# Three due times in a routed attention and gated feed-forward kernel: one pair's loads, one head's one-hot copies, one head's logits

## The chip, the cores and the metric

The kernel runs on one core of one Trainium2 chip. The metric is the device time of one execution in microseconds; the median of three runs is the time of the kernel. In the text, TensorE (PE) does the matmuls, VectorE (DVE), ScalarE (ACT) and GpSimd (POOL) the elementwise work, and SyncE (SP) issues nearly all transfers.

## The reference

```python
q_n, k_n, c_n = (x / (norm(x) + 1e-6) for x in (q, k, centroids))
q_assign = argmax(einsum("bhsd,hcd->bhsc", q_n, c_n), -1)    # 16 clusters a head
k_assign = argmax(einsum("bhsd,hcd->bhsc", k_n, c_n), -1)
mask = q_assign[:, :, :, None] == k_assign[:, :, None, :]
scores = where(mask, q @ k.T / sqrt(64), -1e9)
attn = softmax(scores)                                        # 4 batches, 8 heads, 768 tokens, 64
x = (attn @ v).transpose(0, 2, 1, 3).reshape(3072, 512)
out = (sigmoid(x @ w_gate) * (x @ w_val)) @ w_out             # 512 -> 1536 -> 512
```

Inputs and output are float32. A token attends only to tokens of its head that fall to the same cluster.

## The kernel before

**The mask is part of the score matmul.** For each head a tile `T` holds, for 6 chunks of k and 6 of q, the transposed rows: 64 rows of the values rounded to float16 (`hi`) and 64 rows of what the rounding left (`lo`). `hi` and `lo` together give the cluster logits (`logits`, L354 to L368), on which the cluster is picked (`pick`, L376 to L391): a maximum, a one-hot row for k, and for q a row of -1920 wherever the cluster is not its own. Once the logits of a head are read, 16 of the `lo` rows (64 to 79) are overwritten with these one-hot rows. A score matmul with 80 rows then gives q.k, less 1920 times the mismatch, and an exponential on ACT (L598) makes the weights `es`; an `av` matmul (L611) multiplies them with v and a column of ones.

**How one pair of heads is prepared** (`pair_prep`, L1118 to L1176; in the second, third and fourth batch). SP loads k, q and v of the pair, 384 KB each (`load`, L180). For head e: `sp` casts to `hi` on DVE and subtracts to `lo` on POOL, into a tile `hl` (L1125, L1126); `tn` lets SP issue a DMA transpose of `hl` into `T` (L341); `lg` runs twelve logits matmuls on TensorE (L361), after which ACT or DVE copies one half of them out (`lglo`, L367); `pk` joins and picks on DVE (L373, L382 to L391). When both heads are picked, `ot` issues a DMA transpose of the one-hot tile into `ohT` (L1143), and `hp0` and `hp1` each issue two small copies of 24 KB, from `ohT` into rows 64 to 79 of one head's `T` (`hop`, L412). The score matmuls of the pair need these.

**The order is written by due times.** The attention runs as 384 steps, 96 a batch, each a score matmul of one k chunk against 384 tokens (128 x 384), its exponential, and the `av` of a step two or three earlier. In the second batch head 0 of the third pair begins at step 144, in the third batch the pairs begin at steps 192, 216, 240 and 264. All preparation is put under a due time, the step at which the pair is used plus an offset from the table `SCHED`:

```python
def at(i, f):
    bg.setdefault(max(i, step_no[0] - 0.5), []).append(f)

def run_bg(i):
    for x in sorted(x for x in bg if x <= i):
        for f in bg.pop(x):
            f()
```

`run_bg` is called twice in each step, after the scores and after the `av`. So a due time fixes where an instruction stands in the program and thereby in the in-order list of each engine and queue; it is no wait. What an instruction waits for are its data and the release of the buffer that it writes.

**Between the steps** the feed-forward of 384 tokens that are ready is spread over the steps (`ffn_run`, a budget of ns a step): four matmuls of `g` (L427) and a tanh on ACT (L433), four of `v` (L443) and a product `hT` on DVE (L448), and at the end of a block the matmuls of `o` (L461). Scores, `g`, `v`, logits and `vs_ps` share a ring of four PSUM banks: a new one waits until the bank that it gets has been read out.

**The edited entries,** with their steps before: `b2ld` with `b2lk`, `b2lq`, `b2lv` (loads of all pairs of the third and fourth batch; for the third batch's second pair steps 133, 133.5 and 134.5 for k, q and v), `b1p2hp0` (144 - 10.5 = 133.5; its neighbour `b1p2hp1` stands at 129.5), `b2lg0` and `b2pk0` (for the third batch's first pair 192 - 39 = 153). The transpose of that pair's head 0, `b2tn0`, is due at step 142.

Of the kernel before, what the change touches and what calls it, by code (L numbers as in the profile page):

```python
# [9 lines left out]
HP = mybir.dt.float16  # L10
# [73 lines left out]
}  # L84
# [3 lines left out]
def kernel(  # L88
# [15 lines left out]
    DM = out.shape[1]  # L104
# [10 lines left out]
    PARTS = [(sum(SIZES[:i]), n) for i, n in enumerate(SIZES)]  # L115
    Q0 = SIZES[0]
    NB = 128 * max([3] + SIZES)
    BASE = [0] + [48 * NPT + 96 * (b - 1) for b in range(1, B)]
# [36 lines left out]

    warm = const.tile([128, 512], HP, name="warm")
    POOL.memset(warm, 0.0)
# [37 lines left out]
    def load_half(eng, side, part):  # L195
        if part == 0:
            RAW[side, 0, 0] = raw(side)
        c = slice(3 * part, 3 * part + (3 if side == "k" else Q0))
        eng.dma_start(out=RAW[side, 0, 0][:, 0, c], in_=view(side, 0, 0)[:, 0, c])

    ACT.dma_start(out=cen, in_=centroids.rearrange("h c d -> (h c) d"))
    load_half(SP, "k", 0)
    load_half(ACT, "q", 0)
    load_half(SP, "k", 1)
    load_head(SP, "k", 0, 1)
    load_head(SP, "q", 0, 1, slice(0, Q0))

    WQ = 6
    wg, wv = [], []
    for i in range(NFC // WQ):  # L210
        wg.append(wpool.tile([128, NDC, WQ, 128], HP, name=f"wg{i}"))
        wv.append(wpool.tile([128, NDC, WQ, 128], HP, name=f"wv{i}"))
    wo = [wpool.tile([128, NFC // 2, DM], HP, name=f"wo{i}") for i in range(2)]

# [8 lines left out]
    def load_wo(i):  # L223
        done.add(("wo", i))
        POOL.dma_start(
            out=wo[i],
            in_=moe_w_out.rearrange("(g fc p) m -> p g fc m", g=2, p=128)[:, i],
        )
# [37 lines left out]

    def v_cast(b, p, cast=None):
        done.add(("v", b, p))
        va = VA[b, p] = vas[(b * NP + p) % len(vas)]
        (cast or POOL.tensor_copy)(va[:, :, :, 0:64], RAW["v", b, p])  # L270

# [24 lines left out]

    def v_sum_pe(b, p):
        t = (turns if SCHED.get("lgop", 1) else bank)(130, FP, name="vs_ps")
        for j in range(NCH):
            PE.matmul(  # L300
                out=t.rearrange("p (h d) -> p h d", h=2), lhsT=ones, rhs=VA[b, p][:, :, j, :],
                start=(j == 0), stop=(j == NCH - 1),
            )
        sv = svp.tile([128, 2, 65], FP, tag="sv", name="sv")
        SV[b, p] = sv
        DVE.tensor_scalar(sv.rearrange("p h d -> p (h d)"), t, TINY, None, ALU.mult)
# [35 lines left out]

    def logits2(groups):

        lg = (turns if SCHED.get("lgop", 1) else bank)(512, FP, name="lg2")
        for i, (t, c, h) in enumerate(groups):
            for s in range(2):
                PE.matmul(  # L348
                    out=lg[:, bass.ts(i, NCL)], lhsT=t[:, c, :], rhs=cm[:, h, s, :],
                    start=(i == 0 and s == 0), stop=(s == 1), skip_group_check=True,  # L350
                )
        return lg[:, 0 : len(groups) * NCL].rearrange("p (c n) -> p c n", n=NCL)
# [64 lines left out]
    def ffn_atoms(xT, t0, n, b, ch, final=False):  # L417
# [36 lines left out]
        def outp(t, part, st):  # L454
            def f():
                if part == 0:
                    need(("wo", 0), ("wo", 1))
                    st.append(op.tile([128, DM], FP, tag="o", name="o"))
                o = st[0]
                for fc in range(4 * part, 4 * part + 4):  # L460
                    PE.matmul(  # L461
                        out=o, lhsT=hT[:, fc, bass.ts(t, 128)], rhs=wo[fc // 6][:, fc % 6, :],
                        start=(fc == 0), stop=(fc == NFC - 1),
                    )
# [23 lines left out]
        def closing(t, a, z):  # L488
            def f():
                w = z - a  # L490
                o = bank(w, name="o_end")
                for fc in range(NFC):
                    PE.matmul(  # L493
                        out=o, lhsT=hT[:, fc, bass.ts(t, 128)],
                        rhs=wo[fc // 6][:, fc % 6, a:z],
                        start=(fc == 0), stop=(fc == NFC - 1),
                    )
                ob = osp.tile([128, w], FP, tag="ob_end", name="ob_end")
                if a:
                    DVE.tensor_scalar(ob, o, 0.5, None, ALU.mult)  # L500
                else:
                    ACT.activation(ob, o, AF.Copy, scale=0.5)
                SP.dma_start(
                    out=out[b * S : (b + 1) * S].rearrange("(p c) m -> p c m", c=NCH)[
                        :, ch[t], a:z
                    ],
                    in_=ob,
                )

            return f  # L510
# [90 lines left out]
    def do_av(s):  # L601
        b, p, e, nq = s["b"], s["p"], s["e"], s["nq"]
        first, last = s.get("first", False), s.get("last", False)
        need(("v", b, p))
        if first:
# [58 lines left out]
    def dummies(n, m=512):  # L664
# [3 lines left out]
        for i in range(n):  # L668
            PE.matmul(out=w[:, 0:m], lhsT=warm[:, 0:128], rhs=warm[:, 0:m], start=True, stop=True)

    def pieces(b, p, e, parts=1):
# [107 lines left out]
        return dict(hi=hi, lo=lo, tu=tu, ev=ev, lg=lg, pk=pk, ot=ot, pl=pl)  # L779

    def first(p, e, parts=1):

        h, st = 2 * p + e, {}

        def rng(s, part):
            n = NCH // parts
            return (6, 6 + Q0) if s else (n * part, n * part + n)

# [47 lines left out]
        def lg(part=0):  # L836
# [4 lines left out]
            else:  # L841
                st["lg", part] = logits2(gs)

        def pk(part=0):
# [4 lines left out]
            DVE.tensor_reduce(mx[:, 0:n], lg_, AX.X, ALU.max)  # L849
            m = NCH // parts  # L850
            for s, x, y in ((0, 0, m), (1, m, n)):
                if x == y:
                    continue
                o = m * part if s == 0 else 0
                v_ = oh_view(ohx[0, p], 2 * e + s, 1, 1, 6)[:, 0, o : o + y - x]
# [6 lines left out]
        def ot(part=0):  # L862
            if SCHED.get(f"hO{p}", 0):
# [6 lines left out]
                return  # L870
            n = NCH // parts
            m = n if part else max(n, Q0)
            ps = st["oh", part] = turns(128 * m, name="oh_ps")
            for c in range(m):
                PE.transpose(ps[:, bass.ts(c, 128)], ohx[0, p][:, n * part + c, :], identh)  # L875

        def pl(s, eng=None, part=0):
            a, z = rng(s, part)
            if SCHED.get(f"hO{p}", 0):
                need(f"h{2 * p + 1}ot")  # L880
                hop(ohy[0, p], 2 * e + s, T[0, h], a, z - a)
                return
            src = st["oh", part][64 * e + 32 * s : 64 * e + 32 * s + 16, 0 : 128 * (z - a)]
            dst = T[0, h][64:80, a:z, :].rearrange("p c t -> p (c t)")
# [103 lines left out]
    for x in SCHED.get("lo", ["v0", "k1", "q1", "v1", "k2", "q2", "v2", "k3", "q3", "v3"]):  # L988
        if x[0] == "q":
            load_chunks(SP, "q", int(x[1]), 0)  # L990
# [4 lines left out]
    a, b_ = P[0, 0, 0], P[0, 0, 1]  # L995
    a["hi"](0, None, 0)
    a["hi"](1, ACT.copy, 0)
    a["lo"](0, DVE, 0)
    a["lo"](1, None, 0)
    centroid_b()  # L1000
    a["hi"](0, None, 1)
    a["lo"](0, DVE, 1)
    dummies(SCHED.get("dm1", 3), 128)
    a["tu"](0, 0)
    cv = centroid_c()
    a["tu"](1, 0)
    a["tu"](0, 1)
    a["ev"](0, None, 0)
    a["ev"](1, ACT, 0)
    centroid_d(cv)  # L1010
    a["ev"](0, ACT, 1)
# [22 lines left out]
    def lead_in():  # L1034
# [11 lines left out]
        dummies(SCHED.get("dm3", 8), 128)  # L1046
        a["pl"](0, None, 0)
        a["pl"](1, None, 0)
        slot()
# [4 lines left out]
    at(0, lambda: a["ot"](1))  # L1054
    at(0, lambda: a["pl"](0, None, 1))

# [45 lines left out]
    for p in range(NP):  # L1102
        u = USE[0, p, 0]
        cast = {None: None, "A": ACT.copy, "D": DVE.tensor_copy}[SCHED.get(f"vc0{p}E")]
        plan(f"vc0{p}", u - 12 if p else -4, lambda p=p, cast=cast: v_cast(0, p, cast))
        if SCHED.get(f"vd{p}", 0):
# [5 lines left out]
    for i in range(NFC // WQ):  # L1112
        for j in range(2):
            plan(f"w{i}{j}", 2 + 5 * (2 * i + j), lambda i=i, j=j: load_w(i, j))
    for i in range(2):
        plan(f"wo{i}", 44 + 6 * i, lambda i=i: load_wo(i))

    def pair_prep(b, p, use):  # L1118
# [30 lines left out]
        def go(name, off, f):  # L1149
            o = SCHED.get(f"b{b}p{p}{name}" if b < 2 else f"b2{name}", off)  # L1150

# [26 lines left out]
    for b in range(1, B):  # L1178
        for p in range(NP):
            use = USE[b, p, 0]  # L1180
            o = SCHED.get(f"b1p{p}ld", -76) if b == 1 else SCHED.get("b2ld", -76)
            for side in ("k", "q", "v"):
                d_ = SCHED.get(f"b{min(b, 2)}l{side}" + (f"{p}" if b == 1 else ""), 0)
                at(use + o + d_, lambda b=b, p=p, side=side: load(SP, side, b, p))
            pair_prep(b, p, use)

    lead_in()
    for b in range(B):
# [12 lines left out]
        for p, e, c in heads(b):  # L1201
            for s in head_steps(b, p, e, c):
# [4 lines left out]
                r = step_no[0] - BASE[b]  # L1207
                ns = SCHED.get(f"ns{b}{r // 24}", SCHED.get(f"ns{b}", 500.0))
                ffn_run(ns if b or r >= DONE0[0] else 0.0)
                while len(pend) > LA[min(b, 1)]:  # L1210
# [40 lines left out]
```

## Time and profile before

| | us |
|---|---|
| median of 3 runs | 330.77 (330.39 to 332.48) |
| the profiled execution | 330.29 |
| its span, first to last instruction | 328.3 |
| busy: PE, ACT, DVE, POOL | 321.0, 236.5, 187.1, 108.3 |

A profile is one execution. Busy times are summed over an engine's instructions; rows of a timeline give start, duration, engine, line, operation and what it writes and reads, with the idle time ahead of it and what ended it in square brackets. A wait row gives us in total, the number of times and the longest. The landing time of a transfer runs from its issue to its completion.

### The profile page before, as it was taken

What the parts mean: (1) busy time and instruction counts of PE and PEld (TensorE: products, weight loads), DVE (VectorE), ACT (ScalarE), POOL (GpSimd) and SP (SyncE); (2) the same over time, 40 slices, a digit from 0 to 9 for tenths busy, and PEclk for the clock granted to TensorE, in tenths of its full rate; (3) what the DMA queues carried; (4) which work ended last, traced back from release to release, by engine and by line L of the source; (5) the groups of instructions that cost most, each with busy time, mean ns of one, the idle gap of its engine ahead of it and who ended that gap; (6) DMA issues with size and microseconds to landing.
All of it is one profiled execution on the core that took longest, in us unless ns stands there. A gap on an engine that the chain in (4) does not pass through costs nothing.

```text
span 328.3 us, 8949 instructions
## 1 busy us (share of the span) xinstructions
PE 321.0 (98%) x3405; PEld 208.2 (63%) x3405; DVE 187.1 (57%) x531; ACT 236.5 (72%) x547; POOL 108.3 (33%) x149
## 2 busy tenths in 40 slices
PE   8899999999999999999999999999999999999996
PEld 5788766766666665666566655666566655554654
DVE  6878758787767667556546654666534322441431
ACT  6698988877898888877678767788678876332421
POOL 6875654153435355425133344313301111000000
PEclk9999999999999999999999999999999999999999
DMA  7999996719987896993787473942631012102002
GB/s 215 359 251 217 221 154 112 203 49 248 251 128 192 136 243 134 248 205 72 164 221 116 148 136 80 256 79 50 135 97 36 2 26 76 46 1 86 12 0 96
DMA packets 77994, 45.14 MB, mean 137 GB/s; under 512 B 56896, under 2 KB 75008, under 8 KB 77952
## 3 DMA queue, kind: packets, MB, share of 16 engines
q1 hardware_dynamic: 73984, 39.73, 49.0%
q0 software_dynamic: 3680, 4.72, 8.9%
q8 instruction: 26, 0.43, 0.5%
q14 instruction: 16, 0.13, 0.1%
q10 hardware_dynamic: 288, 0.13, 0.1%
HBM read 28.34 MB, written 6.29 MB: 106 GB/s over the span
## 4 chain that ended last, share of the span: by engine, by line
PE 90%; DMA 4%; ACT 3%; DVE 1%; SPq 1%; issue 1%; POOL 1%
PE g L427 19%; PE v L443 18%; PE o L461 18%; PE sc L593 18%; PE av L611 10%; DMA T<-hl 2%; ACT es L598 2%; PE lg L361 2%; DMA kraw<-in_k_dram 2%; PE o_end L493 1%; PE lg L348 1%; PE oh_ps L875 1%; PE t_ps L821 1%; POOL hl L800 0%; PE sc L590 0%
## 5 line engine op out<-in xcount | busy, mean ns | idle before, releaser
L598 ACT ACTIVATE es<-sc 128x384 f16<-128x384 f32 x384 | 172.7, 494 | 41.5 <-PE sc L593 25.6
L593 PE MATMUL sc<-T 128*128 128x384 f16 x384 | 116.1, 325 | 0.9 <-DMA T<-ohT 0.5
L611 PEld LDWEIGHTS <-es 128*128 128x128 f16 x1152 | 80.2, 98 | 43.0 <-ACT es L598 0.7
L611 PE MATMUL av<-va,es 128*128 128x65 f16 x1152 | 97.4, 194 | 0.3 <-ACT es L598 0.3
L448 DVE SCALAR_TENSOR_TENSOR hT<-th,v 128x384 f16<-128x384 f32 x96 | 53.2, 554 | 66.5 <-PE av L611 43.8
L443 PE MATMUL v<-xTb,wv 128*128 128x384 f16 x384 | 78.1, 326 | 0.0
L427 PE MATMUL g<-xTb,wg 128*128 128x384 f16 x384 | 78.0, 326 | 0.0
L321 POOL TENSOR_TENSOR xp<-t,rec 128x192 f16<-128x192 f32 (+1 forms) x46 | 29.6, 643 | 128.4 <-DVE rec L318 77.5
L461 PE MATMUL o<-wo,hT 128*128 128x512 f16 x276 | 68.7, 379 | 0.0
L433 ACT ACTIVATE th<-g 128x384 f32<-128x384 f32 x96 | 47.2, 492 | 25.7 <-DVE hT L448 17.9
L427 PEld LDWEIGHTS <-wg 128*128 128x128 f16 x384 | 37.1, 97 | 20.9 <-issue 0.6
L443 PEld LDWEIGHTS <-wv 128*128 128x128 f16 x384 | 37.3, 98 | 20.0 <-issue 0.2
L461 PEld LDWEIGHTS <-hT 128*128 128x128 f16 x276 | 26.9, 97 | 23.1
L593 PEld LDWEIGHTS <-T 128*128 128x128 f16 x384 | 37.1, 97 | 1.2 <-DMA T<-ohT 0.6
L316 DVE TENSOR_TENSOR t<-av,sv 128x195 f32<-128x195 f32 (+1 forms) x46 | 20.1, 437 | 25.6 <-PE av L611 20.8
L1126 POOL TENSOR_TENSOR hl<-kraw,hl 128x384 f16<-128x384 f32 x22 | 20.6, 939 | 26.4 <-issue 15.7
L1126 POOL TENSOR_TENSOR hl<-qraw,hl 128x384 f16<-128x384 f32 x22 | 21.6, 984 | 11.8 <-DVE hl L1125 11.8
L373 DVE TENSOR_TENSOR lgs<-lg,lglo 128x192 f32<-128x192 f32 (+1 forms) x25 | 8.7, 348 | 17.7 <-ACT lglo L367 17.2
L470 ACT ACTIVATE ob<-o 128x512 f32<-128x512 f32 x15 | 9.0, 598 | 12.1 <-PE o L461 11.9
L270 POOL CAST va<-vraw 128x768 f16<-128x768 f32 x16 | 13.5, 842 | 1.8 <-DMA vraw<-in_v_dram 1.8
L468 DVE TENSOR_SCALAR ob<-o 128x512 f32<-128x512 f32 x8 | 5.5, 688 | 11.7 <-PE o L461 11.6
L361 PE MATMUL lg<-cm,T 128*128 128x32 f16 x288 | 11.1, 176 | 0.2 <-DMA T<-hl 0.2
(117 smaller groups left out, 243.2 us busy)
## 6 DMA issues: line engine op xcount, KB each, us to landing
vraw<-in_v_dram SPq DMA_DIRECT2D x16, 384.0 KB, 5.1
out_dram<-ob SPq DMA_DIRECT2D x23, 256.0 KB, 2.2
kraw<-in_k_dram SPq DMA_DIRECT2D x15, 384.0 KB, 4.1
qraw<-in_q_dram SPq DMA_DIRECT2D x12, 384.0 KB, 4.3
wg<-in_moe_w_gate_dram POOLq DMA_DIRECT2D x2, 768.0 KB, 9.7
wv<-in_moe_w_val_dram POOLq DMA_DIRECT2D x2, 768.0 KB, 8.6
wo<-in_moe_w_out_dram POOLq DMA_DIRECT2D x2, 768.0 KB, 8.6
qraw<-in_q_dram SPq DMA_DIRECT2D x7, 192.0 KB, 6.8
```

The lines of the kernel that those rows point to most:

```text
L316: DVE.tensor_tensor(t[:, 0:nq, :], av, sv, ALU.add)
L321: (eng or POOL).tensor_tensor(x, t[:, 0:nq, 0:64], bcast(rec[:, 0:nq], 64), ALU.mult)
L361: PE.matmul(out=lg[:, bass.ts(i, 32)], lhsT=t[:, c, :], rhs=cm[:, h].rearrange("p s n -> p (s n)"), start=True, stop=True,)
L427: PE.matmul(out=g[:, 0:n], lhsT=wg[fc // WQ][:, dc, fc % WQ, :], rhs=xT[:, dc, t0 : t0 + n], start=(dc == 0), stop=(dc == NDC - 1),)
L433: ACT.activation(th[:, 0:n], g[:, 0:n], AF.Tanh, scale=0.5)
L443: PE.matmul(out=w[:, 0:n], lhsT=wv[fc // WQ][:, dc, fc % WQ, :], rhs=xT[:, dc, t0 : t0 + n], start=(dc == 0), stop=(dc == NDC - 1),)
L448: DVE.scalar_tensor_tensor(hT[:, fc, 0:n], st[0][:, 0:n], 1.0, w[:, 0:n], ALU.add, ALU.mult)
L461: PE.matmul(out=o, lhsT=hT[:, fc, bass.ts(t, 128)], rhs=wo[fc // 6][:, fc % 6, :], start=(fc == 0), stop=(fc == NFC - 1),)
L593: PE.matmul(out=sc.rearrange("p (c t) -> p c t", t=128), lhsT=s["k"], rhs=s["q"], start=True, stop=True,)
L598: ACT.activation(es, sc, AF.Exp, scale=SCALE)
L611: PE.matmul(out=av[:, s["c0"] + i, :], lhsT=s["es"][:, bass.ts(i, 128)], rhs=VA[b, p][:, e, s["j"], :], start=(first and i == 0), stop=(la ...
L1126: POOL.tensor_tensor(hl[:, :, 64:128], r, hl[:, :, 0:64], ALU.subtract)
```

## The change

The due times of one pair's loads, of one head's copies and of one head's logits and pick move. The loads of the third batch's second pair go from steps 133, 133.5 and 134.5 to 141.5 for all three; the copies `hp0` of the second batch's third pair from 133.5 to 130; logits and pick of head 0 of the third batch's first pair from 153 to 154.5. To name one pair of the later batches, the two look-ups of `SCHED` get one more key.

```diff
-    "b1p2pk1": -27.0, "b1p2ot": -17.5, "b1p2hp0": -10.5, "b1p2hp1": -14.5, "b1p2vc": -18.0,
+    "b1p2pk1": -27.0, "b1p2ot": -17.5, "b1p2hp0": -14, "b1p2hp1": -14.5, "b1p2vc": -18.0,
...
-    "g1pl0E": "A", "hM2": 1, "g1ev0E": "A", "wq": 6,
+    "g1pl0E": "A", "hM2": 1, "g1ev0E": "A", "wq": 6, "b2p1lk": 8, "b2p1lq": 8, "b2p1lv": 8,
+    "b2p0lg0": -37.5, "b2p0pk0": -37.5,
...
         def go(name, off, f):
-            o = SCHED.get(f"b{b}p{p}{name}" if b < 2 else f"b2{name}", off)
+            o = SCHED.get(f"b{b}p{p}{name}", SCHED.get(f"b2{name}", off) if b > 1 else off)
...
                 d_ = SCHED.get(f"b{min(b, 2)}l{side}" + (f"{p}" if b == 1 else ""), 0)
+                d_ = SCHED.get(f"b{b}p{p}l{side}", d_)
                 at(use + o + d_, lambda b=b, p=p, side=side: load(SP, side, b, p))
```

The rest of the diff adds options to the lead-in, the first batch and the weight loads (other orders, other engines, other tile sizes). `SCHED` sets none of them, so that they take the values that the kernel before has fixed; the lines below them move down.

More of the change, by code (lines that the diff above doesn't have):

```diff
@@ L116 @@
     Q0 = SIZES[0]
+    KC = SCHED.get("kc", 3)
     NB = 128 * max([3] + SIZES)
@@ L153, in turns @@
         return op.tile([128, n], dt, tag="o", name=name)
-    warm = const.tile([128, 512], HP, name="warm")
+    WB = SCHED.get("wb", 0)
+    warm = const.tile([128, 128 if WB else 512], HP, name="warm")
     POOL.memset(warm, 0.0)
@@ L197, in load_half @@
             RAW[side, 0, 0] = raw(side)
-        c = slice(3 * part, 3 * part + (3 if side == "k" else Q0))
+        c = slice(0, Q0) if side == "q" else slice(KC, NCH) if part else slice(0, KC)
         eng.dma_start(out=RAW[side, 0, 0][:, 0, c], in_=view(side, 0, 0)[:, 0, c])
-    ACT.dma_start(out=cen, in_=centroids.rearrange("h c d -> (h c) d"))
-    load_half(SP, "k", 0)
-    load_half(ACT, "q", 0)
+    load_cen = lambda: ACT.dma_start(out=cen, in_=centroids.rearrange("h c d -> (h c) d"))
+    if SCHED.get("cq", 0):
+        load_half(SP, "k", 0)
+        load_half(ACT, "q", 0)
+        load_cen()
+    else:
+        load_cen()
+        load_half(SP, "k", 0)
+        load_half(ACT, "q", 0)
     load_half(SP, "k", 1)
@@ L206 @@
     load_head(SP, "q", 0, 1, slice(0, Q0))
-    WQ = 6
+    WQ = SCHED.get("wq", 3)
     wg, wv = [], []
@@ L212 @@
         wv.append(wpool.tile([128, NDC, WQ, 128], HP, name=f"wv{i}"))
-    wo = [wpool.tile([128, NFC // 2, DM], HP, name=f"wo{i}") for i in range(2)]
+    WOP = SCHED.get("wop", 2)
+    WON = NFC // WOP
+    wo = [wpool.tile([128, WON, DM], HP, name=f"wo{i}") for i in range(WOP)]
     def load_w(i, j):
@@ L226, in load_wo @@
             out=wo[i],
-            in_=moe_w_out.rearrange("(g fc p) m -> p g fc m", g=2, p=128)[:, i],
+            in_=moe_w_out.rearrange("(g fc p) m -> p g fc m", g=WOP, p=128)[:, i],
         )
@@ L265, with v_cast @@
         DVE.memset(t[:, :, 64:65], float(NCH))
-    def v_cast(b, p, cast=None):
-        done.add(("v", b, p))
+    def v_cast(b, p, cast=None, e=None):
         va = VA[b, p] = vas[(b * NP + p) % len(vas)]
-        (cast or POOL.tensor_copy)(va[:, :, :, 0:64], RAW["v", b, p])
+        h = slice(0, 2) if e is None else slice(e, e + 1)
+        done.update(("v", b, p, i) for i in range(2)[h])
+        (cast or POOL.tensor_copy)(va[:, h, :, 0:64], RAW["v", b, p][:, h])
     def v_sum(b, p):
@@ L297, in v_sum_pe @@
     def v_sum_pe(b, p):
+        need(("v", b, p, 0), ("v", b, p, 1))
         t = (turns if SCHED.get("lgop", 1) else bank)(130, FP, name="vs_ps")
@@ L341, in turn, with logits2 @@
         SP.dma_start_transpose(out=T[key], in_=hl.rearrange("p c x -> p (c x)"))
-    def logits2(groups):
+    def logits2(groups, sep=False):
         lg = (turns if SCHED.get("lgop", 1) else bank)(512, FP, name="lg2")
[L346 to L351, printed above, removed]
+        lx = sep and SCHED.get("lx", 0)
+        seq = [(i, s) for i in range(len(groups)) for s in range(2)]
+        if lx:
+            seq = [(i, s) for s in range(2) for i in range(len(groups))]
+        for i, s in seq:
+            t, c, h = groups[i]
+            PE.matmul(
+                out=lg[:, bass.ts(i, NCL)], lhsT=t[:, c, :], rhs=cm[:, h, s, :],
+                start=(i == 0 and s == 0), stop=(s == 1), skip_group_check=True,
+            )
         return lg[:, 0 : len(groups) * NCL].rearrange("p (c n) -> p c n", n=NCL)
@@ L456, in f @@
                 if part == 0:
-                    need(("wo", 0), ("wo", 1))
+                    need(*(("wo", i) for i in range(WOP)))
                     st.append(op.tile([128, DM], FP, tag="o", name="o"))
@@ L461, in f @@
                     PE.matmul(
-                        out=o, lhsT=hT[:, fc, bass.ts(t, 128)], rhs=wo[fc // 6][:, fc % 6, :],
+                        out=o, lhsT=hT[:, fc, bass.ts(t, 128)], rhs=wo[fc // WON][:, fc % WON, :],
                         start=(fc == 0), stop=(fc == NFC - 1),
@@ L494, in f @@
                         out=o, lhsT=hT[:, fc, bass.ts(t, 128)],
-                        rhs=wo[fc // 6][:, fc % 6, a:z],
+                        rhs=wo[fc // WON][:, fc % WON, a:z],
                         start=(fc == 0), stop=(fc == NFC - 1),
@@ L603, in do_av @@
         first, last = s.get("first", False), s.get("last", False)
-        need(("v", b, p))
+        need(("v", b, p, e))
         if first:
@@ L668, in dummies @@
         for i in range(n):
-            PE.matmul(out=w[:, 0:m], lhsT=warm[:, 0:128], rhs=warm[:, 0:m], start=True, stop=True)
+            if WB:
+                PE.matmul(
+                    out=w[:, 0:m].rearrange("p (a c) -> p a c", c=128), lhsT=warm,
+                    rhs=warm.unsqueeze(1).to_broadcast([128, m // 128, 128]), start=True, stop=True,
+                )
+            else:
+                PE.matmul(out=w[:, 0:m], lhsT=warm[:, 0:128], rhs=warm[:, 0:m], start=True, stop=True)
     def pieces(b, p, e, parts=1):
@@ L779, in pieces, with BOTH @@
         return dict(hi=hi, lo=lo, tu=tu, ev=ev, lg=lg, pk=pk, ot=ot, pl=pl)
+    ohps = {}
+    def BOTH(p):
+        return p > 0 and SCHED.get(f"oP{p}", 0)
     def first(p, e, parts=1):
@@ L785, in rng @@
         def rng(s, part):
-            n = NCH // parts
-            return (6, 6 + Q0) if s else (n * part, n * part + n)
+            if s:
+                return 6, 6 + Q0
+            return (0, NCH) if parts == 1 else ((0, KC), (KC, NCH))[part]
         def hi(s, eng=None, part=0):
@@ L841, in lg @@
             else:
-                st["lg", part] = logits2(gs)
+                st["lg", part] = logits2(gs, h == 0 and part == 0)
         def pk(part=0):
@@ L849, in pk @@
             DVE.tensor_reduce(mx[:, 0:n], lg_, AX.X, ALU.max)
-            m = NCH // parts
+            k0, k1 = rng(0, part)
+            m = k1 - k0
             for s, x, y in ((0, 0, m), (1, m, n)):
@@ L853, in pk @@
                     continue
-                o = m * part if s == 0 else 0
+                o = k0 if s == 0 else 0
                 v_ = oh_view(ohx[0, p], 2 * e + s, 1, 1, 6)[:, 0, o : o + y - x]
@@ L870, in ot @@
                 return
-            n = NCH // parts
-            m = n if part else max(n, Q0)
+            if BOTH(p):
+                if e == 0:
+                    return
+                need(f"h{h - 1}pk")
+            k0, k1 = rng(0, part)
+            m = k1 - k0 if part else max(k1, Q0)
             ps = st["oh", part] = turns(128 * m, name="oh_ps")
+            ohps[p] = ps
             for c in range(m):
-                PE.transpose(ps[:, bass.ts(c, 128)], ohx[0, p][:, n * part + c, :], identh)
+                PE.transpose(ps[:, bass.ts(c, 128)], ohx[0, p][:, k0 + c, :], identh)
         def pl(s, eng=None, part=0):
@@ L882, in pl @@
                 return
+            if BOTH(p):
+                need(f"h{2 * p + 1}ot")
+                st["oh", part] = ohps[p]
             src = st["oh", part][64 * e + 32 * s : 64 * e + 32 * s + 16, 0 : 128 * (z - a)]
@@ L988 @@
     for x in SCHED.get("lo", ["v0", "k1", "q1", "v1", "k2", "q2", "v2", "k3", "q3", "v3"]):
-        if x[0] == "q":
+        if x == "v0" and SCHED.get("v0h", 0):
+            RAW["v", 0, 0] = raw("v")
+            load_head(SP, "v", 0, 0)
+        elif x == "y0":
+            if SCHED.get("v0h", 0):
+                load_head(SP, "v", 0, 1)
+        elif x[0] == "q":
             load_chunks(SP, "q", int(x[1]), 0)
@@ L996 @@
     a["hi"](0, None, 0)
+    if SCHED.get("cb", 0):
+        centroid_b()
     a["hi"](1, ACT.copy, 0)
     a["lo"](0, DVE, 0)
-    a["lo"](1, None, 0)
-    centroid_b()
-    a["hi"](0, None, 1)
+    a["lo"](1, DVE if SCHED.get("ql", 0) else None, 0)
+    if not SCHED.get("cb", 0):
+        centroid_b()
+    if SCHED.get("tx", 0):
+        a["tu"](0, 0)
+        if SCHED.get("tx", 0) == 2:
+            a["ev"](0, None, 0)
+    a["hi"](0, POOL.tensor_copy if SCHED.get("kp", 0) else None, 1)
+    if SCHED.get("tx", 0) == 3:
+        a["ev"](0, None, 0)
     a["lo"](0, DVE, 1)
     dummies(SCHED.get("dm1", 3), 128)
-    a["tu"](0, 0)
-    cv = centroid_c()
+    if SCHED.get("cc", 0):
+        cv = centroid_c()
+    if not SCHED.get("tx", 0):
+        a["tu"](0, 0)
+    if not SCHED.get("cc", 0):
+        cv = centroid_c()
     a["tu"](1, 0)
     a["tu"](0, 1)
-    a["ev"](0, None, 0)
+    if SCHED.get("cd", 0):
+        centroid_d(cv)
+    if SCHED.get("tx", 0) < 2:
+        a["ev"](0, None, 0)
     a["ev"](1, ACT, 0)
-    centroid_d(cv)
+    if not SCHED.get("cd", 0):
+        centroid_d(cv)
     a["ev"](0, ACT, 1)
@@ L1046, in lead_in @@
         dummies(SCHED.get("dm3", 8), 128)
-        a["pl"](0, None, 0)
-        a["pl"](1, None, 0)
+        a["pl"](0, ACT if SCHED.get("lq", 0) else None, 0)
+        a["pl"](1, ACT if SCHED.get("lp", 0) else None, 0)
         slot()
@@ L1054 @@
     at(0, lambda: a["ot"](1))
-    at(0, lambda: a["pl"](0, None, 1))
+    at(0, lambda: a["pl"](0, ACT if SCHED.get("lr", 0) else None, 1))
     def put(nm, key, u, off, f, arg):
@@ L1104 @@
         cast = {None: None, "A": ACT.copy, "D": DVE.tensor_copy}[SCHED.get(f"vc0{p}E")]
-        plan(f"vc0{p}", u - 12 if p else -4, lambda p=p, cast=cast: v_cast(0, p, cast))
+        if p == 0 and SCHED.get("v0h", 0):
+            plan("vc00", -4, lambda: v_cast(0, 0, cast, 0))
+            plan("vcy0", -3, lambda: v_cast(0, 0, None, 1))
+        else:
+            plan(f"vc0{p}", u - 12 if p else -4, lambda p=p, cast=cast: v_cast(0, p, cast))
         if SCHED.get(f"vd{p}", 0):
@@ L1114 @@
             plan(f"w{i}{j}", 2 + 5 * (2 * i + j), lambda i=i, j=j: load_w(i, j))
-    for i in range(2):
+    for i in range(WOP):
         plan(f"wo{i}", 44 + 6 * i, lambda i=i: load_wo(i))
@@ L1208 @@
                 ns = SCHED.get(f"ns{b}{r // 24}", SCHED.get(f"ns{b}", 500.0))
+                ns += SCHED.get(f"nx{step_no[0]}", 0)
                 ffn_run(ns if b or r >= DONE0[0] else 0.0)
```

## The prediction

> **What bounds the kernel now.** I read the page first, then the stretches of time, then TensorE's waits.
>
> ```profile
> span 328.3 us, 8949 instructions
> PE 321.0 (98%) x3405; PEld 208.2 (63%) x3405; DVE 187.1 (57%) x531; ACT 236.5 (72%) x547; POOL 108.3 (33%) x149
> ```
>
> Busy time by stretch of the span, with the granted clock, the DMA share and GB/s at the end of each row:
>
> ```profile
> core 0: us, PE busy (x) PEld busy (x) DVE busy (x) ACT busy (x) POOL busy (x), PEclk, DMA share, GB/s
> 50.00:100.00 50.00, 49.94 (x586) 33.31 (x584) 37.49 (x104) 42.48 (x98) 19.36 (x25) 1.00 0.72 162
> 100.00:112.00 12.00, 11.18 (x135) 7.53 (x134) 7.78 (x25) 9.98 (x24) 5.05 (x6) 1.00 0.96 203
> 112.00:150.00 38.00, 37.69 (x411) 24.06 (x410) 23.96 (x71) 31.30 (x76) 15.96 (x19) 1.00 0.79 185
> 150.00:200.00 50.00, 50.00 (x498) 31.07 (x496) 27.88 (x78) 36.87 (x87) 16.58 (x19) 1.00 0.64 146
> ```
>
> TensorE's waits between 100 and 112 us (two rows) and between 130 and 140 us (the last), in us, times and longest:
>
> ```profile
> PE sc L593 <- DMA T<-ohT: 0.5, 1, 0.5
> PE lg L361 <- DMA T<-hl: 0.2, 1, 0.2
> PE av L611 <- ACT es L598: 0.3, 1, 0.3
> ```
>
> TensorE sets the time: it is 98% busy, its granted clock is 1.00 in every stretch, and from 50 to 100 us and from 150 to 200 us it has no idle time worth naming. The exception is 100 to 112 us, with 12.00 - 11.18 = 0.82 us idle. Two waits fill it: a score matmul waits for the copy of one-hot rows out of ohT, and a group of logits matmuls waits for the transposed tile T<-hl. Both are late transfers; the whole question is whether the change removes these two waits and whether it makes new ones. The 0.3 us wait on an exponential comes 20 us later and is not touched.
>
> The busy figure hides part of each wait, since the rows of pipelined matmuls overlap. So I read the starts, in TensorE's timeline (start, duration):
>
> ```profile
> 102.84 0.25 PE L611 MATMUL av<-va,es 128*128 128x65 f16 x3
> 103.62 0.32 PE L593 MATMUL sc<-T 128*128 128x384 f16 x1 [0.52 <-DMA T<-ohT]
> ...
> 108.95 0.26 PE L611 MATMUL av<-va,es 128*128 128x65 f16 x3
> 109.44 0.47 PE L361 MATMUL lg<-cm,T 128*128 128x32 f16 x12 [0.24 <-DMA T<-hl]
> 109.76 0.32 PE L593 MATMUL sc<-T 128*128 128x384 f16 x1
> 109.92 0.81 PE L427 MATMUL g<-xTb,wg 128*128 128x384 f16 x4
> 110.57 0.25 PE L611 MATMUL av<-va,es 128*128 128x65 f16 x3
> 110.66 0.32 PE L593 MATMUL sc<-T 128*128 128x384 f16 x1
> ...
> 113.48 0.32 PE L593 MATMUL sc<-T 128*128 128x384 f16 x1
> ```
>
> After three av matmuls the next instruction starts 0.09 us behind their start (110.57 to 110.66). So the score of step 144 was due at 102.84 + 0.09 = 102.93 and started at 103.62: **0.69 us lost**. The logits were due at 108.95 + 0.09 = 109.04 and started at 109.44: **0.40 us lost**. Together 1.09 us, where the idle column shows 0.52 + 0.24 = 0.76. The Trainium skill warns of this (Perfetto Trace Analysis, Identifying the Most-Contended Engine): matmul busy share is a poor measure of headroom, as pipelined matmuls look different in the trace. By the idle column the prize would be 0.76 us, by the starts it is 1.09; the starts are measured, so I take them.
>
> **Why the two transfers are late.** SP's queue is in order, and around 100 us it is nearly back to back (start, duration of the issue):
>
> ```profile
> 97.51 1.55 SPq L412 DMA_DIRECT2D T<-ohT  x2
> 99.12 0.72 SPq L182 DMA_DIRECT2D kraw<-in_k_dram  x1
> 99.89 1.14 SPq L412 DMA_DIRECT2D T<-ohT  x2
> 101.07 0.58 SPq L182 DMA_DIRECT2D qraw<-in_q_dram  x1
> 101.70 0.47 SPq L182 DMA_DIRECT2D vraw<-in_v_dram  x1
> 102.27 2.58 SPq L341 DMA_TRANSPOSE T<-hl  x1
> ```
>
> The landing rows of single issues among them, in KB and us from issue to landing: the second copy of the first pair, the first copy of the second pair, k, v and the transpose.
>
> ```profile
> T<-ohT SPq DMA_DIRECT2D x1, 24.0 KB, 1.8
> ...
> T<-ohT SPq DMA_DIRECT2D x1, 24.0 KB, 3.4
> ...
> kraw<-in_k_dram SPq DMA_DIRECT2D x1, 384.0 KB, 4.0
> ...
> vraw<-in_v_dram SPq DMA_DIRECT2D x1, 384.0 KB, 4.7
> ...
> T<-hl SPq DMA_TRANSPOSE x1, 7.1
> ```
>
> And from GpSimd's timeline the last subtraction ahead of the transpose:
>
> ```profile
> 101.15 0.92 POOL L1126 TENSOR_TENSOR hl<-qraw,hl 128x384 f16<-128x384 f32 x1 [0.69 <-DVE hl L1125]
> ```
>
> The copies of head 0's rows (the pair at 99.89) stand behind a 384 KB load of k. The pair ahead of that load lands in about 1.8 us a copy, the pair behind it in up to 3.4. The transpose T<-hl goes out at 102.27, since the subtraction that fills hl ends at 101.15 + 0.92 = 102.07, and lands at 102.27 + 7.1, about 109.4.
>
> **The change, part by part.** No instruction is added or removed on any engine. In the instruction order POOL's list is unchanged, DVE's differs in buffer names only, and SP, TensorE and ACT each change in one place.
>
> *Loads eight steps later and copies 3.5 steps sooner.* Steps only order the program; SP does not wait for them, it issues when it is free. Between the old and the new place of the loads stands no SP instruction other than the two copies: k goes behind them, and q and v stay just behind k and ahead of the transpose. The copies moved forward pass the same k load. So both edits do the same thing, and either would do it alone: the order copies, k, copies, q, v, T becomes copies, copies, k, q, v, T. The raw buffers that the loads refill are long free (no wait on an engine stands on them), and first use of the loaded k is at step 158, over 16 steps on, so a load about 1.1 us later costs nothing; without that slack it would cost these 1.1 us.
>
> The pair is then issued from 99.12 to 99.12 + 1.14 = 100.26. With 1.8 us it lands near 101.5 to 102.1, with 3.4 us, now that no load stands ahead, at most near 103.0 (second issue about 99.6). It is due at 102.93. I take 1.8, the row of the pair with no load ahead of it: the wait is gone, **-0.69 us** (other end: -0.62).
>
> k is issued about 100.3, and q, v and T<-hl follow at 101.1, 101.7 and 102.27 as before: T still waits for the subtraction. The bytes ahead of T are the same, so it should still land at 109.4.
>
> *Logits of head 0 of the third batch 1.5 steps later.* Twelve matmuls move past one score, one gate group, one av group and one more score. Their new place with no wait: the score behind them moves up to 109.04, the gate to 109.20, av to 109.85, the next score to 109.94, logits at 110.10; less the 0.69 that is won, 109.41. T lands at 109.4. So the second wait goes too, **-0.40 us**, with nearly nothing to spare: each 0.1 us by which T is later comes back as 0.1 us of wait. Without the move the logits would be due at 109.04 - 0.69 = 108.35 and would wait 1.05 us, giving the first gain back.
>
> What it moves in turn: ACT copies lglo behind one more exponential, and DVE's join, pick and mask of these logits come later against TensorE, with a hT product queued behind them.
>
> ```profile
> 109.95 0.32 ACT L367 COPY lglo<-lg 128x192 f32<-128x192 f32 x1 [0.30 <-PE lg L361]
> ...
> 110.77 0.49 ACT L433 ACTIVATE th<-g 128x384 f32<-128x384 f32 x1
> 111.16 0.87 ACT L598 ACTIVATE es<-sc 128x384 f16<-128x384 f32 x2
> ...
> 110.30 0.36 DVE L373 TENSOR_TENSOR lgs<-lg,lglo 128x192 f32<-128x192 f32 x1 [0.78 <-ACT lglo L367]
> ...
> 111.54 0.19 DVE L391 TENSOR_SCALAR oh<-oh 128x96 f16<-128x96 f16 x1
> 111.99 0.56 DVE L448 SCALAR_TENSOR_TENSOR hT<-th,v 128x384 f16<-128x384 f32 x1 [0.26 <-PE av L611]
> ```
>
> The gate's row now ends at 109.20 - 0.69 + 0.81 = 109.32, th starts at 109.36, the exponential 0.39 behind it, lglo 0.39 later at 110.14, the join at 110.14 + 0.35 = 110.49. Join to mask took 111.73 - 110.30 = 1.43 us, so hT starts near 111.9 and ends near 112.45. Its matmuls are done earlier than that: hT, ahead of which DVE idled for 0.26 us, is now late, and with it the PSUM bank of its v. In the changed kernel's instruction list the score that waits for that bank is the one that stood at 113.48, now due at 113.48 - 1.09 = 112.39. So it waits between 0 and 0.2 us; I take **+0.1**, as hT ends just behind the due time. What follows hT on DVE (the sum for v, the normalising add, hl) is up to 1.2 us late against TensorE and finds idle time before the next join.
>
> **Sum.** -0.69 - 0.40 + 0.1 = -1.0 us on the profiled execution, which took 330.29 (span 328.3 and 2.0 around it). The median of the three runs is 330.77, 0.48 above it, their lowest 330.39. I start from halfway, 330.5, and forecast **329.5 us**, a gain of 0.3%.
>
> **The rivals.**
>
> *The bank comes free too late.* Mechanism as above, but hT holds up the score of step 161 and the pick holds the logits' bank for the gate before it: price up to 0.6 us, the delay of hT against the next idle DVE time. For: DVE is in order and the pick is 1.43 us long. Against: these scores leave a bank more time than before in the new order. Time: 330.5 - 1.09 + 0.6 = 330.0.
>
> *The copies do not land sooner,* so that the change does not do what it says: 3.4 us were due to something other than the load ahead. Then only the logits' wait goes: 330.5 - 0.4 = 330.1. Against: the other pair's 1.8.
>
> *Slower: the transpose lands behind three loads in a row.* T<-hl took 7.1 us with two loads just ahead of it; the median of all 24 is 3.9:
>
> ```profile
> T<-hl SPq DMA_TRANSPOSE x24, 3.9
> 103.00:104.00 1.00, 0.48 (x9) 0.32 (x6) 0.97 (x3) 0.16 (x2) 0.27 (x1) 1.00 0.68 186
> ```
>
> That is 1.6 us a load. If k, now 1.1 us closer, counts as a third, T lands at 111.0 and the logits wait 111.0 - 109.41 = 1.6 us: 330.5 - 1.09 + 1.6 = 331.0. It is slower from a landing at 109.41 + 1.09 = 110.5 on. For: k would land at 100.3 + 4.0 = 104.3, inside T's time. Against: the engines were only 0.68 busy from 103 to 104 us, while q was about to start, so k finds room; v landed at 106.4, well ahead of T. The Trainium skill (DMA: Bandwidth & Descriptors, Queues, rings and completion order) says that a transfer's completion lands only after every earlier write of the same DMA engine; that speaks for this rival, and the 3.4 beside 1.8 agrees with it.
>
> **How the numbers follow.** Forecast 0.65; transpose behind three loads 0.15; bank late 0.1; copies no sooner 0.06; something I do not see 0.04. Range: low end, all of the 0.82 + 0.31 idle from 100 to 150 us and the hidden 0.33 gone from 330.29, 328.9; high end the slower rival, 331.0. One per cent, 3.3 us, is about what a measurement of this kernel can tell from no change. No case comes near it: TensorE's idle time behind 100 us and ahead of the tail is 1.1 us, so faster 0.02; a cascade of new waits is left for slower, 0.04; within, 0.94.
>
> **What would show it.** Right: on SP two pairs of copies in a row, then k, q, v; no wait of sc on T<-ohT near 103 us; T<-hl still landing near 7 us after issue; logits without a wait near 109.4; TensorE busy over 11.9 of 12 us in that stretch. Wrong: T<-hl landing 8 us or more after issue, or a score some 3 us behind the logits that starts late against its neighbours, with hT ended just before it.

## The result and the profile after

| | before | after |
|---|---|---|
| median, us | 330.38 | 329.42 |
| ratio of the two, 95% interval | | 0.9970 (0.9959 to 0.9981) |
| span of the profiled execution, us | 328.3 | 327.5 |

Both kernels ran 22 times here; before's 330.77 in the prediction is the median of its first three runs. One run of before took 665.57 us, which moves its median by less than 0.01 us. The gain is 0.96 us, 0.3%, and its interval (0.6 to 1.4 us) is clear of no change.

The two waits are gone. TensorE's busy time in the stretch that had 0.82 us of idle time (columns as before, sum of busy time per engine, clock, DMA share, GB/s):

```profile
100.00:112.00 12.00, 11.94 (x144) 8.13 (x143) 7.58 (x23) 10.80 (x27) 5.33 (x6) 1.00 0.95 205
```

11.18 us have become 11.94. In the changed file the score matmuls stand at L610, `av` at L628 and the logits at L378. In TensorE's timeline the score of step 144 and the logits stand right behind their neighbours:

```profile
103.14 0.25 PE L628 MATMUL av<-va,es 128*128 128x65 f16 x3
103.23 0.33 PE L610 MATMUL sc<-T 128*128 128x384 f16 x1
...
109.57 0.32 PE L610 MATMUL sc<-T 128*128 128x384 f16 x1
109.73 0.45 PE L378 MATMUL lg<-cm,T 128*128 128x32 f16 x12
110.03 0.25 PE L628 MATMUL av<-va,es 128*128 128x65 f16 x3
...
112.60 0.25 PE L628 MATMUL av<-va,es 128*128 128x65 f16 x3
112.74 0.32 PE L610 MATMUL sc<-T 128*128 128x384 f16 x1
```

The first gap is 0.09 us, which is the usual spacing, where it had been 0.78; the logits follow their score by 0.16. The last two rows show the one new loss: 0.14 in place of 0.09, so 0.05 us.

SP's queue after, and the landing rows (KB, us from issue to landing) of the second copy of head 0 and of the transpose:

```profile
97.56 3.10 SPq L429 DMA_DIRECT2D T<-ohT  x4
100.70 0.58 SPq L185 DMA_DIRECT2D kraw<-in_k_dram  x1
101.34 0.46 SPq L185 DMA_DIRECT2D qraw<-in_q_dram  x1
101.84 0.47 SPq L185 DMA_DIRECT2D vraw<-in_v_dram  x1
102.42 2.98 SPq L354 DMA_TRANSPOSE T<-hl  x1
```

```profile
T<-ohT SPq DMA_DIRECT2D x1, 24.0 KB, 1.9
...
T<-hl SPq DMA_TRANSPOSE x1, 6.9
```

All four copies go out in a row, then k, q, v, with no pause of eight steps (some 6 us) ahead of the loads. The copies land in about 2 us where they had taken up to 3.4; the transpose lands as late as before, at 102.42 + 6.9 = 109.3, and nobody waits for it.

### The profile page after: what moved, and what is told of

It is laid out like the page before. It is cut to its first block, busy times and chain, and to the rows that moved or that the text cites. A ratio compares the mean times of both kernels' runs of the same rounds, so it can differ in the third digit from the quotient of the medians.

```text
span 327.5 us, 8945 instructions
## 1 busy us (share of the span) xinstructions
PE 321.2 (98%) x3405; PEld 208.7 (64%) x3405; DVE 186.8 (57%) x531; ACT 236.3 (72%) x547; POOL 108.2 (33%) x149
## 4 chain that ended last, share of the span: by engine, by line
PE 94%; DMA 2%; ACT 1%; SPq 1%; POOL 1%; DVE 0%; issue 0%
PE g L444 19%; PE v L460 19%; PE sc L610 19%; PE o L478 18%; PE av L628 11%; PE lg L378 2%; DMA kraw<-in_k_dram 2%; PE lg L365 1%; ACT es L615 1%; PE t_ps L850 1%; PE o_end L510 1%; PE oh_ps L910 1%; PE sc L607 1%; POOL hl L829 0%; PE vs_ps L313 0%; PE t_ps L733 0%
## 5 line engine op out<-in xcount | busy, mean ns | idle before, releaser
L610 PE MATMUL sc<-T 128*128 128x384 f16 x384 | 116.1, 325 | 0.4 <-DVE T L935 0.2
L628 PEld LDWEIGHTS <-es 128*128 128x128 f16 x1152 | 80.1, 98 | 42.9 <-ACT es L615 0.7
L628 PE MATMUL av<-va,es 128*128 128x65 f16 x1152 | 97.4, 194 | 0.3 <-ACT es L615 0.3
L610 PEld LDWEIGHTS <-T 128*128 128x128 f16 x384 | 37.0, 96 | 0.6 <-DVE T L935 0.4
L378 PE MATMUL lg<-cm,T 128*128 128x32 f16 x288 | 11.0, 176 | 0.0
```

Source lines behind the costliest of these rows:

```text
L378: PE.matmul(out=lg[:, bass.ts(i, 32)], lhsT=t[:, c, :], rhs=cm[:, h].rearrange("p s n -> p (s n)"), start=True, stop=True,)
L610: PE.matmul(out=sc.rearrange("p (c t) -> p c t", t=128), lhsT=s["k"], rhs=s["q"], start=True, stop=True,)
L628: PE.matmul(out=av[:, s["c0"] + i, :], lhsT=s["es"][:, bass.ts(i, 128)], rhs=VA[b, p][:, e, s["j"], :], start=(first and i == 0), stop=(la ...
```

## The experiments

All have the entries of the kernel before, apart from those named (the sixth starts from the fifth). They are set in the changed kernel's file, so lines are numbered as there. Each ratio is against the kernel before in runs on the same chip.

**1. The copies alone.**

```diff
-"b1p2hp0": -10.5
+"b1p2hp0": -14
```

> Only the copies hp0 are due 3.5 steps sooner; loads and logits stay. Theory (two waits in a row on transfers): the score's wait on T<-ohT near 103 us goes (0.69 us by starts, 0.52 in the idle column), but the logits then stand 0.69 us earlier in front of a transpose that lands when it did, so their wait grows from 0.40 to between 0.7 and 1.05 us: net gain 0 to 0.35 us, 330.0 to 330.4. Rival (the two gains are independent): -0.69 us, 329.7, with the logits' wait unchanged at 0.2 in the idle column.

Measured 330.37 us against 330.45, ratio 0.9997 (0.9984 to 1.0009). TensorE's timeline at the logits:

```profile
109.00 0.25 PE L628 MATMUL av<-va,es 128*128 128x65 f16 x3
110.08 0.47 PE L378 MATMUL lg<-cm,T 128*128 128x32 f16 x12 [0.82 <-DMA T<-hl]
```

SP issues the four copies in a row from 97.97 us and k behind them at 100.84. There is no wait on T<-ohT any more, but the logits are due at 109.09 and start at 110.08: 0.99 us lost, where the two waits of before were 0.69 and 0.40. The gain of the first wait is handed to the second. The rival of independent gains (329.7) falls.

**2. The loads alone.**

```diff
+"b2p1lk": 8, "b2p1lq": 8, "b2p1lv": 8
```

> Only the three loads are due at step 141.5; copies and logits stay. Theory (a due time is an order, not a pause): SP's order becomes copies, copies, k, q, v, T as with the copies moved, so profile and time are those of the copies alone: no wait on T<-ohT near 103 us, logits waiting 0.7 to 1.05 us, k issued near 100.5 us. Rival (the loads really go out eight steps, some 6 us, later): k issued near 105 us, T<-hl landing in about 4 us instead of 7, both waits gone, 329.3.

Measured 330.92 us against 330.45, ratio 1.0011 (0.9992 to 1.003). SP's queue, then TensorE's timeline:

```profile
97.47 2.95 SPq L429 DMA_DIRECT2D T<-ohT  x4
100.46 0.58 SPq L185 DMA_DIRECT2D kraw<-in_k_dram  x1
```

```profile
108.48 0.25 PE L628 MATMUL av<-va,es 128*128 128x65 f16 x3
109.72 0.46 PE L378 MATMUL lg<-cm,T 128*128 128x32 f16 x12 [0.99 <-DMA T<-hl]
```

k is issued at 100.46, not 6 us later, behind four copies in a row, as in the first experiment; the logits lose 109.72 - 108.57 = 1.15 us. Moving the loads back is the same edit of the queue as moving the copies forward. The higher median is not shown to be the edit's: five of the twelve executions had a mean granted clock of 0.993 to 0.995 and took 331.11 to 331.94 us (of before, on the same chip, seven of 35 had such a clock; of the first experiment none), and the other seven have a median of 330.35 us, the same as the first experiment within 0.02.

**3. The logits alone.**

```diff
+"b2p0lg0": -37.5, "b2p0pk0": -37.5
```

> Only logits and pick of the one head are due 1.5 steps later. Theory: the score's wait on T<-ohT stays (0.52 in the idle column), the logits' wait goes, as they are due at 110.1 us against a landing near 109.4: -0.40 us, 330.0. Rival (the later pick holds hT and with it a PSUM bank): a wait of a score on hT some 3 us behind the logits of up to 0.6 us, no gain, 330.4 to 330.6.

Measured 330.15 us against 330.45, ratio 0.999 (0.9967 to 1.0012). The size, 0.3 us, agrees, but the interval holds both no gain and the 0.40 us; the profile decides. Its only wait on a transfer in this stretch is that of the score:

```profile
103.29 0.25 PE L628 MATMUL av<-va,es 128*128 128x65 f16 x3
103.85 0.32 PE L610 MATMUL sc<-T 128*128 128x384 f16 x1 [0.30 <-DMA T<-ohT]
```

103.85 - 103.38 = 0.47 us lost, the logits lose nothing.

**4. Copies and logits, loads as before.**

```diff
-"b1p2hp0": -10.5
+"b1p2hp0": -14
+"b2p0lg0": -37.5, "b2p0pk0": -37.5
```

> Copies and logits as in the changed kernel, the loads as before. Theory (the loads' due time is redundant): the same order on every engine and queue as the changed kernel, hence its time, 329.4, and no wait on T<-ohT or T<-hl near 103 and 109 us. Rival (the loads carry part of the gain): between 329.4 and 330.4, with T<-hl landing later than 7 us after issue.

Measured 329.67 us against 330.45, ratio 0.9981 (0.9969 to 0.9992); 11.94 of 12 us busy from 100 to 112 us, as in the changed kernel. The loads' due time adds nothing that shows. The profiled execution is the longest of its twelve, 330.83 us: its granted clock fell near 12 us (the last section shows it), while from 100 to 112 us it was 1.00.

**5. The loads behind the transpose, logits in their old place.**

```diff
-"b1p2hp0": -10.5
+"b1p2hp0": -14
+"b2p1lk": 9.5, "b2p1lq": 9.5, "b2p1lv": 9.5
```

> Copies as in the changed kernel, logits at their old place, the three loads due at step 143, so that SP issues them behind the transpose T<-hl. Theory (the 7 us of T<-hl are the q and v loads ahead of it): T<-hl lands in about 4 us, near 106.5, the logits due near 108.4 wait for nothing, and the logits' move is not needed: gain 1.0 to 1.1 us, 329.3 to 329.4; k now lands near 109 us, long ahead of step 158. Rival (the wait only goes further): the next transpose of the pair, issued near 108.8, now has the loads ahead of it and lands in 7 us, near 115.8, where its logits are due near 114.9: a new wait of up to 0.9 us there, 329.9 to 330.3. Second rival (the 7 us are the transpose's own): T<-hl still lands in 7 us, logits wait 1.0 us, 330.4.

Measured 329.76 us against 330.46, ratio 0.998 (0.997 to 0.9989). SP's queue, the transpose's landing row, and the logits:

```profile
97.89 3.07 SPq L429 DMA_DIRECT2D T<-ohT  x4
102.44 1.44 SPq L354 DMA_TRANSPOSE T<-hl  x1
103.93 0.88 SPq L185 DMA_DIRECT2D kraw<-in_k_dram  x1
```

```profile
T<-hl SPq DMA_TRANSPOSE x1, 4.0
```

```profile
108.63 0.25 PE L628 MATMUL av<-va,es 128*128 128x65 f16 x3
108.72 0.46 PE L378 MATMUL lg<-cm,T 128*128 128x32 f16 x12
109.03 0.32 PE L610 MATMUL sc<-T 128*128 128x384 f16 x1
109.26 0.81 PE L444 MATMUL g<-xTb,wg 128*128 128x384 f16 x4
```

With no load ahead the transpose lands in 4.0 us, and the logits start on time in their old place; the gate matmuls behind them start 0.23 us after their score instead of 0.16, a small loss of 0.07. With q and v just ahead the transpose took 6.5 to 7.4 us in six profiles (before, the changed kernel, the first four experiments). So the loads made it late, and there are two ways to the same gain: logits later, or loads behind the transpose. The next transpose, now with the loads ahead of it, landed in 4.9 us and nobody waited for it.

**6. As the fifth, with the logits moved too.**

```diff
+"b2p0lg0": -37.5, "b2p0pk0": -37.5
```

> As the run before it, with the logits 1.5 steps later as in the changed kernel. Theory: no wait for either transfer is left to remove, so the same time within 0.1 us: 329.3 to 329.5; the only difference is a wait of a score of 0.05 us on hT some 3 us behind the logits. Rival (the later pick matters): slower than the run before it by 0.3 us or more.

Measured 329.63 us against 330.46, ratio 0.9978 (0.9966 to 0.9991): the same as the fifth and as the changed kernel. With both waits gone the move adds nothing that shows. Here the transpose took 5.4 us with no load ahead, so the fifth's 4.0 is one value out of a spread; the wait is gone with either.

**7. The copies behind all three loads.**

```diff
-"b1p2hp0": -10.5
+"b1p2hp0": -9
```

> Loads and logits as in the kernel before, the copies of head 0 due 1.5 steps later, so that SP issues them behind all three loads. Theory (each load ahead of the copies delays them): they go out near 101.1 to 102.2 us, 1.2 us later than before, and land behind q and v too, 3.4 to 5 us after issue, near 105 to 106: the score waits 2 to 3 us in place of 0.69, and the logits' 0.40 vanishes behind it, as T<-hl then goes out near 103.4 and lands near 110.5 while the logits are due near 111: net 1.0 to 2.5 us slower, 331.4 to 332.9. Rival (the copies are small and pass the loads): 1.2 us later at most, minus the 0.40: 331.2 or less.

Measured 334.2 us against 330.46, ratio 1.0109 (1.0083 to 1.0136), 3.6 us slower by the ratio and beyond both expectations. The wait is about as forecast: the score is due at 102.96 and starts at 105.88, 2.92 us lost, 2.23 more than before, and the 0.40 at the logits is gone. That makes 1.8 us. The rest stands in the stretches and in the matmuls behind the wait:

```profile
103.00:105.88 2.88, 0.12 (x4) 0.03 (x1) 1.05 (x4) 0.17 (x1) 0.91 (x1) 1.00 1.18 297
105.88:107.00 1.12, 1.12 (x8) 0.65 (x9) 0.00 (x0) 0.76 (x2) 0.00 (x0) 0.70 1.05 230
107.00:108.00 1.00, 1.00 (x7) 0.50 (x6) 0.00 (x0) 0.34 (x2) 0.00 (x0) 0.50 0.00 0
...
110.00:111.00 1.00, 0.95 (x13) 0.58 (x11) 0.96 (x4) 0.72 (x2) 0.00 (x0) 1.00 0.05 11
```

```profile
106.29 1.44 PE L444 MATMUL g<-xTb,wg 128*128 128x384 f16 x4
107.53 0.37 PE L628 MATMUL av<-va,es 128*128 128x65 f16 x3
...
108.50 1.43 PE L460 MATMUL v<-xTb,wv 128*128 128x384 f16 x4
109.76 0.26 PE L628 MATMUL av<-va,es 128*128 128x65 f16 x3
```

After 2.75 us without work TensorE's granted clock falls to 0.50 and is back at 1.00 by 110 us. Four matmuls take 1.24 and 1.26 us from start to next start instead of 0.65; over all instructions from 106.29 to 109.76 that is some 1.7 us more than at full clock. 1.8 + 1.7 = 3.5 us. From the `av` group at 98.84 to the gate behind the logits, at 113.50, this trace needs 14.66 us, where before needs 109.92 - 98.81 = 11.11: 3.55 us more, and the ratio gives 3.6. Two of the six executions had a mean clock of 1.000 and 0.999 and took 332.36 and 333.07 us, the first within the forecast for the wait alone, the second 0.2 us above it. So the fall of the clock is not in every execution of this edit.

**8. The copies behind two loads.**

```diff
-"b1p2hp0": -10.5
+"b1p2hp0": -10
```

> Loads and logits as in the kernel before, the copies of head 0 due half a step later, so that SP issues them behind the loads of k and q and ahead of v. Theory (each load ahead of the copies delays them, and TensorE's clock halves only after an idle time of nearly 3 us, as with the copies behind all three loads): the copies land near 104.5 us, the score waits 1.4 to 1.9 us by starts in place of 0.69, the logits not at all, the granted clock stays 1.00: +0.3 to +0.8 us against before, 330.8 to 331.3. Rival (an idle time of half that is enough for the clock to fall): granted clock near 0.5 for some 3 us behind the wait, 1.7 us more: 332.5 to 333.

Measured 331.48 us against 330.8, ratio 1.0025 (1.0007 to 1.0042), 0.8 us slower. The stretches and the wait:

```profile
103.00:105.00 2.00, 0.45 (x6) 0.23 (x3) 1.37 (x5) 0.49 (x2) 0.91 (x1) 1.00 1.00 315
105.00:107.00 2.00, 1.61 (x18) 1.12 (x19) 0.18 (x1) 1.22 (x3) 0.00 (x0) 1.00 1.23 278
```

```profile
103.19 0.26 PE L628 MATMUL av<-va,es 128*128 128x65 f16 x3
105.39 0.32 PE L610 MATMUL sc<-T 128*128 128x384 f16 x1 [1.95 <-DMA T<-ohT]
```

105.39 - 103.28 = 2.11 us lost, 0.2 more than expected; less 0.69 and 0.40 that makes 1.0 us, within the interval (0.2 to 1.4 us). In this execution the clock stays at 1.00. Three others of the twelve had a mean clock of 0.995 and took 332.43 to 333.10 us, about the time that the rival gives; of before, on the same chip, one of 17 had such a clock (0.994). Whether theirs fell behind this wait or elsewhere no trace shows, so the rival is not refuted.

Copies behind no load, one, two and three loads of 384 KB thus cost TensorE 0, 0.69, 2.11 and 2.92 us of waiting by starts, and landed in about 1.9, up to 3.4, up to 4.1 and up to 4.6 us. In the last two cases part of the wait is a later issue, by some 1.1 us: the two copies go out from 101.0 us, where before they did from 99.9.

## Why the prediction was right

*The two waits and their size.* The prize was read from the starts, 1.09 us, not from the idle column, 0.76. Over the whole stretch the starts bear this out: from the same av group, at 98.81 before and 99.11 after, to the one ahead of the later logits, at 115.67 and 114.92, the changed kernel needs 15.81 us instead of 16.86, **1.05 us less**. By the idle column it would be 0.76, the change in busy time. The spans differ by 0.8 only, because that profiled execution was already 0.30 us late at 99 us, ahead of anything that moved; the medians differ by 0.96. The forecast is closer than its parts: the start value, 330.5, was 0.12 us above the median of before and the gain, 1.0, 0.04 above the measured one, and the two errors partly cancel.

*The copies.* The row chosen for them, 1.8 us, fits (1.8 to 2.2 measured); the wait is gone whole.

*Steps are an order.* That the loads would not go out later by eight steps, and that either edit alone would turn the queue, is shown by the first, second and fourth experiments.

*The second wait grows if the first goes alone.* The text gave 1.05 us; the first two experiments have 0.99 and 1.15. This is why the logits' move carries the whole net gain, although alone it is worth only some 0.3 us: the three edits are not additive.

*The transpose.* It was to stay near 7 us, landing just as the logits are due. It landed at 109.3 with the logits at 109.73, so 0.4 us were to spare in that execution. By the prediction's own times the two met within 0.01 us; nearly all of the spare time came from TensorE being 0.30 us late there, and the landing times of 6.5 to 7.4 us spread by more, so that this profile has no wait is partly luck. In the fourth experiment, with the same order, the transpose landed at 103.90 + 6.5 = 110.4 and the logits started at 111.25. That the transpose waits for the subtraction is borne out: in the fifth experiment SP was free from 97.89 + 3.07 = 100.96 and issued it only at 102.44. The slower rival, three loads at 1.6 us each ahead of the transpose, is not borne out: with k closer it took 6.9, not the 8.7 that the rival adds up. Its price per load was too simple: with v alone just ahead the transpose took 4.5 us in the eighth experiment, with none 4.0 and 5.4, and with all three ahead, but the two copies between, 4.3 in the seventh. What sets the size stays open; that the loads just ahead make it late is what the runs show.

*The bank.* Given as 0 to 0.2 with 0.1 taken, it measured 0.05. Its chain is as described: the join starts late and hT ends just before the score that needs the bank.

```profile
110.79 0.36 DVE L390 TENSOR_TENSOR lgs<-lg,lglo 128x192 f32<-128x192 f32 x1 [1.65 <-ACT lglo L384]
...
112.14 0.55 DVE L465 SCALAR_TENSOR_TENSOR hT<-th,v 128x384 f16<-128x384 f32 x1
```

hT ends at 112.69 and the score starts at 112.74. The 0.14 stands in the profiles of the experiments that move the logits (third, fourth, sixth) and 0.09 to 0.10 in the first, second and fifth, so the loss is this move's; that the bank is what the score waits for no row says, it follows from the order of the instructions and these two times.

*Two small slips.* The low end adds up to 330.29 - 0.82 - 0.31 - 0.33 = 328.83, not 328.9. And 1% is not what a measurement here can tell from no change: with 22 runs each the interval of the gain is 0.6 to 1.4 us, 0.2% wide.

*What was missed* is the price of going wrong. The prediction left 0.04 for a slowdown by over 1% as a cascade of new waits; the seventh experiment shows a plainer way there, one wait of 2.9 us and, in the profiled execution, a clock that falls after it.

## What to carry to other kernels

When an engine is full but for two waits on transfers, take both edges at once: removing the first only moves the idle time to the second, unless the second's data come sooner too (the fifth experiment) or are needed later (the changed kernel). Read the lost time from starts against the usual spacing, since pipelined rows hide part of it. In a queue that nothing paces, ask which transfer stands ahead of which, not at what step it was written. And look at the granted clock of every execution before a difference of a microsecond is put down to an edit.

## What the runs showed of the hardware

An idle time of 2.75 us on TensorE cost more than itself: in the seventh experiment's profile the granted clock fell from 1.00 to 0.50 near 106.3 us, less than 0.5 us after work came back, and stayed there for 3.4 us, some 1.7 us lost on top of the wait; after 1.95 us idle, in the eighth experiment's profile, it stayed at 1.00. The Trainium skill (TensorE: Matmul & The Clock Gate, Part 1) describes half clock after an idle window of about 3.4 us that runs freely. The half clock agrees (0.50), but here an idle time shorter than one such window was enough.

The length of an idle time does not decide alone. In the fourth experiment's profile the clock fell to 0.50 near 11.7 us and stayed there for 3.4 us too. The clock by slices of 8.2 us, in tenths, and the longest wait of TensorE from 2 to 16 us:

```profile
PEclk9799999999999999999999999999999999999999
...
PE t_ps L850 <- POOL hl L829: 0.4, 1, 0.4
```

No idle time above 0.40 us stands ahead of this fall, and TensorE was 0.73 to 0.95 busy in each microsecond from 6 to 11. The profile of before has a wait of 0.47 us and TensorE only 0.53 busy from 10 to 11 us, and its clock stayed at 1.00.

One such stretch, 3.4 us at half clock in some 330, takes about 0.005 off the mean clock of an execution. Read so, four of the seventh experiment's six executions had one or two (mean clock 0.995 and 0.994, twice 0.989) and two had none. Where those fell that were not profiled is not known. So no safe idle time and no limit between 1.95 and 2.75 us is shown; what decides stays open.
